# One dense pass inside each P V burst, as eight strip products, in a layer of local attention and a feed-forward gate

## The chip, the cores and the metric

The kernel runs on one core of a Trainium2 chip. The metric is the device time of the whole program in microseconds; a kernel's time is the median of its runs. Beside it stands one execution taken by the hardware profiler, whose span (first to last instruction of the program) and rows are quoted.

## The reference

One layer over 2048 tokens of width 448, in bf16. x is normalized to xn. Branch A is causal attention with 16 heads of 28 over eight positions two apart, the token's own and seven before it; branch B is a feed-forward layer of width 1792 with gelu. The result is x plus the product of the first with silu of the second:

```python
qkv = (xn @ wqkv).reshape(B, S, 3, H, Dh)
idx = pos[:, None] - 2 * arange(8)[None, :]          # masked where negative
attn = softmax(einsum("bhsd,bhswd->bhsw", q, k[idx]) * Dh ** -0.5)
s = einsum("bhsw,bhswd->bhsd", attn, v[idx]) @ wo
g = silu(gelu(xn @ w1 + b1) @ w2 + b2)
return x + s * g
```

## The kernel before, in words

**Tokens and stages.** Tokens of even and odd position are kept apart, so that the neighbours two apart lie side by side; there are 16 tiles of 128 tokens in 4 chunks of 4 tiles. For each tile: statistics and normalization (L422 to L507), a transposed copy xnT, projections to q, k (`qk_rows`, L569) and v (`vproj`, L592). For each chunk: ff1 (`ff1`, L645), that is 14 row tiles of the hidden layer over 512 tokens, evacuated by ScalarE with gelu (L655); ff2 (`ff2`, L671), evacuated into the gate (`gate`, L712). Last the output projection and the gated sum (`final`, L857; `gated`, L881) and the DMA out (L900). For tiles in TWICE (8, 9, 10) that DMA is issued in two halves.

**Attention** goes over nine blocks of up to 228 tokens. A visit S(b) is a *score burst* (`scores_of`, L740): 32 products of 64x128 with 57 columns (L750), then exp on ScalarE (L759) and a mask on VectorE (L765). A visit P(b) is a *P V burst* (`values_of`, L769): 64 products with 57 columns, in the mode in which the 128x128 array stands as eight tiles of 64 rows and 32 columns (L779). Four loops go over s (four quarters of the block), g (column strip of 32), h, and a (row half); so the first 32 products are s = 0 and 1. The row halves write two banks. VectorE then transposes (L791), divides (L795, L799), and turns the result into oT (L816); GpSimd and ScalarE move pieces (L812). Bursts are numbered by their block, 0 to 8.

**The dense pair.** All large products but the first and the last tiles go through `pair` (L514). It takes two jobs a and b (two tiles of the same kind) and runs them beside each other in the two row halves of the array (64x128 mode): a on the upper 64 rows of its contraction with bank p, b on the lower 64 rows with bank q; then the halves are swapped. One *pass* is two such products side by side. A q/k, v or ff1 pair has four passes before the swap and three after, an ff2 pair 7 + 7 and 7 + 7, an output projection three and four. Since after the swap another row half writes into the same bank, the first swapped products wait for a `nop` on GpSimd (`told`, L534), which waits for the last products before the swap (`behind`, L510). The weight slices are `half_rows` (L454).

**The order of the work** is written out by hand. The kernel first makes a list of tasks (`plan.add`), each with an engine, dependencies, and buffers taken and given back (`_Pool`; the eight PSUM banks are `p_b`); `plan.run` places them in the sequence of the list ORDER (a negative number takes the task's second engine), with a cost model that only fixes which free buffer a task gets; `plan.emit` issues them in that sequence, each engine's queue in its own part of it. A pool `p_f` with a CLK task of 3.5 keeps P V bursts apart in the plan. TensorE's task for a P V burst is made in `attn` (L838, task at L849).

Of the kernel before, what the change touches and what calls it, by code (L numbers as in the profile page):

```python
# [13 lines left out]
HOP = 0.10  # L14
TABLE = 1.28
SWITCH = 0.095
AT_ONCE = ("DMA", "CLK")
BURST = 3.5
ORDER = [
# [42 lines left out]
]  # L62
LAST = 352
TWICE = (8, 9, 10)
# [126 lines left out]
def kernel(  # L191
# [13 lines left out]
    P = 128  # L205
# [308 lines left out]
    def pair(a, b, early=False, before=(range(4),), after=(range(3),), late=((),), give=()):  # L514
        held, size = {}, sum(map(len, before)) + sum(map(len, after))

        def part(j, ps, kt, half, n):
            return lambda: j.part(ps, kt, half, n == 0, n == size - 1)

        n, t = 0, None  # L520
        for i, ks in enumerate(before):
            def f1(k, ks=ks, n=n):
                p, q = buf(p_b, t, 0), buf(p_b, t, 1)
                held["last"] = together([part(a, p, kt, 0, n + m) for m, kt in enumerate(ks)], [part(b, q, kt, 1, n + m) for m, kt in enumerate(ks)])[-1]
            u = plan.add("PE", pe(a.n, len(ks)), f1, (list(late[i]) + [u] if i else a.deps + b.deps + a.late + b.late),
                         take=() if i else (p_b, p_b) + a.into + b.into, tail=0.15, mode=64)
            t = t or u
            n += len(ks)
# [7 lines left out]
        for i, ks in enumerate(after):  # L536
            def f3(k, ks=ks, n=n, i=i):
                p, q = buf(p_b, t, 0), buf(p_b, t, 1)
                for x in together([part(b, q, kt, 0, n + m) for m, kt in enumerate(ks)], [part(a, p, kt, 1, n + m) for m, kt in enumerate(ks)])[0]:
                    if not i:  # L540
                        behind(x, held["told"])
            u = plan.add("PE", pe(a.n, len(ks)), f3, [u if i else told], give=give if i + 1 == len(after) else (), tail=0.15, mode=64)
            n += len(ks)
# [25 lines left out]
    def qk_rows(t, which):  # L569
        cs = slice(t * P, (t + 1) * P)  # L570

        def part(ps, kt, half, start, stop):
            r = half_rows(half)
            w = w_in[r, kt, which * D:(which + 1) * D] if kt < 3 else w_in3[r, 0, :]
            return nc.tensor.matmul(ps[:, :D], xnT[r, kt, cs], w, start=start, stop=stop)  # L575
# [16 lines left out]
    def vproj(t):  # L592
        k0 = t * P

        def part(ps, kt, half, start, stop):
            r = half_rows(half)
            w = w_in[r, kt, 2 * D:] if kt < 3 else w_in3[r, 1, :]
            return nc.tensor.matmul(ps[:, :D], xnT[r, kt, k0:k0 + P], w, start=start, stop=stop)  # L598
# [46 lines left out]
    def ff1(c, mt, gate):  # L645
# [3 lines left out]
        def part(ps, kt, half, start, stop):  # L649
            r = half_rows(half)  # L650
            return nc.tensor.matmul(ps[:], w1[r, kt, ms], xnT[r, kt, cs], start=start, stop=stop)  # L651
# [19 lines left out]
    def ff2(t):  # L671
# [5 lines left out]
        elif t % 2 == 0:  # L677
            def job(t):
                cs = slice(t % TPC * P, t % TPC * P + P)

                def part(ps, mt, half, start, stop):
                    r = half_rows(half)
                    return nc.tensor.matmul(ps[:, :D], buf(*h_at[(c, mt)])[r, cs], w2[r, mt, :], start=start, stop=stop)  # L683
# [384 lines left out]
```

## Time and profile before

| what | us |
|---|---|
| runs | 150.19, 150.27, 150.95 |
| median | 150.27 |
| the profiled execution | 150.79 |
| its span | 149.1 |
| TensorE busy in the span | 144.4 |
| VectorE, ScalarE, GpSimd busy | 107.0, 102.9, 27.8 |

In the profile PE is TensorE's products, PEld its weight loads, DVE VectorE, ACT ScalarE, POOL GpSimd, SP the engine that issues most DMAs; L651 is line 651 of the kernel. Times are in microseconds unless marked ns. A group's row has the engine, the operation, the tiles written and read, their shapes and the count, then busy time and the mean of one in ns. Rows of a timeline give the start, the length up to the end of the last instruction, and the count. The start of a product is recorded; its end is modelled.

### The profile page before, as it was taken

The numbers are of one execution on the slowest core, as the hardware profiler recorded it, in microseconds if no ns is written. First come the engines' busy times: TensorE is split into PE (matmuls) and PEld (weight loads), VectorE is DVE, ScalarE is ACT, GpSimd is POOL, SyncE is SP. The second block draws the span as 40 slices with busy tenths as digits, with TensorE's granted clock in tenths as the row PEclk, the third lists the DMA queues.
The fourth block names the chain that finished last, engine by engine and source line by source line (L and its number), as shares of the span: only waits on it lengthen the run. The fifth ranks groups of instructions, "written<-read, shape, count | busy, mean of one in ns | idle before, by whom it ended". The sixth has DMA issues, their size and how long they took to land.

```text
span 149.1 us, 5240 instructions
## 1 busy us (share of the span) xinstructions
PE 144.4 (97%) x2158; PEld 74.5 (50%) x2158; DVE 107.0 (72%) x271; ACT 102.9 (69%) x187; POOL 27.8 (19%) x84
## 2 busy tenths in 40 slices
PE   7899999999999999999999999999999999999991
PEld 2445444444455555556555655445565444454461
DVE  2775640635545877975997897997979969899473
ACT  3255996878779687937968687988974588642720
POOL 6123230005174002314101011041020210200000
PEclk9999999999999999999999999999999999999999
DMA  4999996998857958699875587520303001030122
GB/s 153 306 280 323 194 133 166 228 346 171 103 99 179 154 129 96 201 163 198 214 85 131 169 115 177 109 65 6 91 22 94 2 4 31 1 95 31 31 66 64
DMA packets 39222, 19.47 MB, mean 131 GB/s; under 512 B 25815, under 2 KB 38586, under 8 KB 39198
## 3 DMA queue, kind: packets, MB, share of 16 engines
q1 hardware_dynamic: 38510, 18.10, 58.9%
q0 software_dynamic: 544, 0.91, 2.4%
q8 instruction: 17, 0.28, 0.8%
q10 hardware_dynamic: 144, 0.11, 0.3%
q14 instruction: 7, 0.06, 0.1%
HBM read 9.42 MB, written 3.94 MB: 90 GB/s over the span
## 4 chain that ended last, share of the span: by engine, by line
PE 94%; DMA 2%; DVE 2%; issue 0%; ACT 0%
PE bank L651 29%; PE bank L683 25%; PE bank L575 15%; PE bank L598 7%; PE bank L867 6%; PE bank L779 4%; PE bank L705 4%; PE bank L750 3%; DMA x_sb<-in_A_x_dram 2%; PE bank L875 1%; DVE st L424 1%; PE bank L499 1%; DVE xn L464 0%; DVE sg L887 0%; ACT w_in L724 0%
## 5 line engine op out<-in xcount | busy, mean ns | idle before, releaser
L651 PE MATMUL bank<-xnT,w 64*128 64x512 bf16 x392 | 44.8, 376 | 0.0
L655 ACT ACTIVATE h<-bank,b 128x512 bf16<-128x512 f32 x56 | 35.4, 690 | 8.1 <-PE bank L651 6.8
L683 PE MATMUL bank<-w,h 64*128 64x448 bf16 x392 | 39.9, 349 | 0.0
L651 PEld LDWEIGHTS <-w 64*128 64x128 bf16 x392 | 18.7, 94 | 22.2
L683 PEld LDWEIGHTS <-h 64*128 64x128 bf16 x392 | 18.3, 94 | 16.3
L575 PE MATMUL bank<-w_in,xnT 64*128 64x448 bf16 (+1 forms) x212 | 25.8, 349 | 0.0
L759 ACT ACTIVATE E<-bank 128x456 bf16<-128x456 f32 (+1 forms) x36 | 17.5, 554 | 3.7 <-PE bank L750 3.6
L313 ACT CAST qk_tok<-bank 128x448 bf16<-128x448 f32 x27 | 13.4, 536 | 7.1 <-PE bank L575 5.0
L424 DVE BATCH_NORM_STATS2 st<-x_sb 128x6 f32<-128x448 bf16 x16 | 9.6, 609 | 10.4 <-DMA x_sb<-in_A_x_dram 10.4
L791 DVE STREAM_TRANSPOSE wide<-bank 128x512 f32<-128x512 f32 x18 | 12.3, 702 | 5.1 <-PE bank L779 5.1
L575 PEld LDWEIGHTS <-xnT 64*128 64x128 bf16 (+1 forms) x212 | 10.6, 94 | 10.2 <-issue 0.8
L812 POOL COPY wide<-wide 64x64 bf16<-64x64 bf16 x23 | 6.6, 305 | 47.4 <-PE bank L651 19.3
L598 PE MATMUL bank<-w_in,xnT 64*128 64x448 bf16 (+1 forms) x106 | 13.6, 350 | 0.0
L816 DVE STREAM_TRANSPOSE oT<-wide 128x512 bf16<-128x512 bf16 x18 | 12.2, 694 | 0.7 <-POOL wide L812 0.5
L464 DVE TENSOR_SCALAR xn<-x_sb,mv,rstd 128x448 bf16<-128x448 bf16 x16 | 6.1, 391 | 8.2 <-POOL rstd L446 8.0
L765 DVE TENSOR_TENSOR E<-E,m_gen 128x456 bf16<-128x456 bf16 (+1 forms) x32 | 11.7, 378 | 0.1
L717 DVE TENSOR_TENSOR wide<-bank,b 128x448 f32<-128x448 f32 x15 | 8.9, 615 | 3.9 <-PE bank L683 2.2
L867 PE MATMUL bank<-wo,oT 64*128 64x448 bf16 x98 | 11.6, 349 | 0.0
L799 DVE TENSOR_TENSOR wide<-wide,rd 128x448 bf16<-128x448 f32 x18 | 11.2, 626 | 0.4
L635 ACT ACTIVATE kd<-qkT,head 128x1024 bf16<-128x1024 bf16 x10 | 11.2, 1157 | 0.0
L313 ACT CAST v_tok<-bank 128x448 bf16<-128x448 f32 x13 | 6.6, 537 | 4.6 <-issue 3.9
L729 ACT ACTIVATE wide<-wide 128x448 f32<-128x448 f32 x12 | 7.0, 579 | 3.2 <-DVE wide L717 3.1
(81 smaller groups left out, 138.9 us busy)
## 6 DMA issues: line engine op xcount, KB each, us to landing
v<-v_hbm SPq DMA_DIRECT2D x16, 128.0 KB, 2.8
v_hbm<-v_tok SPq DMA_DIRECT2D x15, 128.0 KB, 3.6
w<-in_B_w_dram SPq DMA_DIRECT2D x2, 672.0 KB, 7.8
out_dram<-o SPq DMA_DIRECT2D x12, 112.0 KB, 1.7
w_in<-in_A_wqkv_dram SPq DMA_DIRECT2D x3, 336.0 KB, 5.4
x_sb<-in_A_x_dram SPq DMA_DIRECT2D x4, 224.0 KB, 2.7
w<-in_B_w_dram SPq DMA_DIRECT2D x2, 448.0 KB, 5.5
w<-in_B_w_dram SPq DMA_DIRECT2D x2, 336.0 KB, 6.3
```

The lines of the kernel that those rows point to most:

```text
L313: nc.scalar.copy(o, i)
L575: return nc.tensor.matmul(ps[:, :D], xnT[r, kt, cs], w, start=start, stop=stop)
L598: return nc.tensor.matmul(ps[:, :D], xnT[r, kt, k0:k0 + P], w, start=start, stop=stop)
L635: nc.scalar.activation(dst, src, ACT.Copy, scale=head[:, a:a + 1])
L651: return nc.tensor.matmul(ps[:], w1[r, kt, ms], xnT[r, kt, cs], start=start, stop=stop)
L655: nc.scalar.activation(buf(p_h, own, i)[:], buf(p_b, own, i)[:], ACT.Gelu_apprx_tanh, bias=b1[:, mt:mt + 1])
L683: return nc.tensor.matmul(ps[:, :D], buf(*h_at[(c, mt)])[r, cs], w2[r, mt, :], start=start, stop=stop)
L759: nc.scalar.activation(buf(p_E, k)[:, :8 * n], buf(p_b, a, at + i)[:, :8 * n], ACT.Exp, scale=SCALE)
L765: nc.vector.tensor_tensor(out=E, in0=E, in1=m[:, :, :, :n].rearrange("p i g q -> p (i g) q"), op=ALU.mult)
L791: nc.vector.transpose(buf(p_dt, k)[:], buf(p_b, po, a)[:])
L816: nc.vector.transpose(oT[:, a::2, q:q + 256], turned_in(d[a]).rearrange("p l b c -> p l (b c)"))
L867: return nc.tensor.matmul(ps[:, :D], oT[r, kt, t * P:(t + 1) * P], wo[r, kt, :], start=start, stop=stop)
```

## The change

One pass of nine dense pairs is taken out of its pair's task and issued between the second and the third quarter (s = 2) of a P V burst, in P V's own tiling mode: each of its two 64x128 products becomes four products of 64x32, one for each column strip (`product` with a strip, `strips` in `pair`). The strips of the two row halves alternate, so eight products fill the eight tiles of the array; they write 32 partitions each of the pair's two banks. The table INSIDE says for each burst from which pair the pass comes, whether from before or after the swap (0 or 1), and from which part: burst 0 the first pass of tile 8's q/k pair, burst 1 the first swapped pass of the v pair of tiles 10 and 11, burst 2 the same of ff2's tiles 2 and 3, burst 3 the first pass of the second part of ff2's tiles 6 and 7, bursts 4, 7 and 8 the first swapped pass of an ff1 pair, bursts 5 and 6 the first pass of ff2's tiles 8 and 10.

Where that pass is the pair's first, a HOLD task without cost takes the pair's two banks ahead of the burst. Where it is the first after the swap, the first two strip products carry the wait for `told`. The pair's remaining passes come behind the burst, or, if the pass isn't the pair's first, the earlier part ahead of it. The burst's task keeps its cost of 0.52 in the plan; the pair's task is planned with a pass less.

ORDER is another list of 922 entries throughout. TWICE becomes empty, so tiles 8, 9 and 10 go out in one DMA each. The diff, without ORDER and with the repeated edits of `part` shown once:

```diff
+INSIDE = {
+    0: (("qk", 8), 0, 0), 1: (("v", 10), 1, 0), 2: (("ff2", 2), 1, 0), 3: (("ff2", 6), 0, 1), 4: (("ff1", 2, 1), 1, 0),
+    5: (("ff2", 8), 0, 0), 6: (("ff2", 10), 0, 0), 7: (("ff1", 3, 2), 1, 0), 8: (("ff1", 3, 6), 1, 0),
+}
...
-TWICE = (8, 9, 10)
+TWICE = ()
...
-    def pair(a, b, early=False, before=(range(4),), after=(range(3),), late=((),), give=()):
+    def product(ps, n, lhsT, rhs, start, stop, strip=None):
+        rows = slice(0, P) if strip is None else slice(32 * strip, 32 * strip + 32)
+        return nc.tensor.matmul(ps[rows, :n], lhsT[:, rows], rhs, start=start, stop=stop)
+
+    t_pv, in_pv, ahead_of_pv, behind_pv = {}, {}, {}, {}
+
+    def put_inside(b, deps, fn):
+        in_pv[b] = fn
+        if b in t_pv:
+            t_pv[b].deps += deps
+            return [t_pv[b]]
+        ahead_of_pv[b] = deps
+        return None
+
+    def pair(a, b, name, early=False, before=(range(4),), after=(range(3),), late=((),), give=()):
         held, size = {}, sum(map(len, before)) + sum(map(len, after))
...
+        def strips(t, kt, n, swap):
+            x, y = (b, a) if swap else (a, b)
+            p, q = buf(p_b, t[0], int(swap)), buf(p_b, t[0], 1 - int(swap))
+            return [i for j in range(4) for i in together([part(x, p, kt, 0, n, j)], [part(y, q, kt, 1, n, j)])[0]]
...
         for i, ks in enumerate(before):
+            deps = list(late[i]) + [u] if i else a.deps + b.deps + a.late + b.late
+            take = () if i else (p_b, p_b) + a.into + b.into
+            visit, wait = places.get((0, i)), None
+            if visit is not None:
+                if not i:
+                    t = plan.add("HOLD", 0.0, None, deps, take=take, tail=-HOP)
+                    deps, take = [t], ()
+                wait = put_inside(visit, deps, lambda kt=ks[0], n=n: strips(own, kt, n, False))
+                deps, ks, n = wait or [], ks[1:], n + 1
...
         for i, ks in enumerate(after):
+            deps = [u if i else told]
+            visit, wait = places.get((1, i)), None
+            if visit is not None:
+                def f(kt=ks[0], n=n, i=i):
+                    for x in strips(own, kt, n, True)[:2]:
+                        if not i:
+                            behind(x, held["told"])
+                wait = put_inside(visit, deps, f)
+                deps, ks, n = wait or [], ks[1:], n + 1
...
-            return nc.tensor.matmul(ps[:, :D], xnT[r, kt, cs], w, start=start, stop=stop)
+            return product(ps, D, xnT[r, kt, cs], w, start, stop, strip)
...
             for s in range(4):
+                if s == 2 and b in in_pv:
+                    in_pv[b]()
                 for g in range(G):
...
-        a = plan.add("PE", 0.52, lambda k: fn([buf(p_b, k, i) for i in range(2)]), masked + t_v[b] + last_visit[what][-1:],
+        a = plan.add("PE", 0.52, lambda k: fn([buf(p_b, k, i) for i in range(2)]), masked + t_v[b] + last_visit[what][-1:] + ahead_of_pv.get(b, []),
                      take=(p_b, p_b, p_f), give=give, tail=0.15, mode=33)
+        t_pv[b] = a
+        if b in behind_pv:
+            behind_pv[b].deps.append(a)
```

More of the change, by code (lines that the diff above doesn't have):

```diff
@@ L524, in f1 @@
                 held["last"] = together([part(a, p, kt, 0, n + m) for m, kt in enumerate(ks)], [part(b, q, kt, 1, n + m) for m, kt in enumerate(ks)])[-1]
-            u = plan.add("PE", pe(a.n, len(ks)), f1, (list(late[i]) + [u] if i else a.deps + b.deps + a.late + b.late),
-                         take=() if i else (p_b, p_b) + a.into + b.into, tail=0.15, mode=64)
+            u = plan.add("PE", pe(a.n, len(ks)), f1, deps, take=take, tail=0.15, mode=64)
+            if visit is not None and not wait:
+                behind_pv[visit] = u
             t = t or u
+            own[:] = [t]
             n += len(ks)
@@ L536, in pair, with f3 @@
         for i, ks in enumerate(after):
-            def f3(k, ks=ks, n=n, i=i):
+            deps = [u if i else told]
[7 more added lines that the diff above has]
+                deps, ks, n = wait or [], ks[1:], n + 1
+            def f3(k, ks=ks, n=n, i=i, first=not i and visit is None):
                 p, q = buf(p_b, t, 0), buf(p_b, t, 1)
                 for x in together([part(b, q, kt, 0, n + m) for m, kt in enumerate(ks)], [part(a, p, kt, 1, n + m) for m, kt in enumerate(ks)])[0]:
-                    if not i:
+                    if first:
                         behind(x, held["told"])
-            u = plan.add("PE", pe(a.n, len(ks)), f3, [u if i else told], give=give if i + 1 == len(after) else (), tail=0.15, mode=64)
+            u = plan.add("PE", pe(a.n, len(ks)), f3, deps, give=give if i + 1 == len(after) else (), tail=0.15, mode=64)
+            if visit is not None and not wait:
+                behind_pv[visit] = u
             n += len(ks)
@@ L570, in qk_rows, with part @@
         cs = slice(t * P, (t + 1) * P)
-        def part(ps, kt, half, start, stop):
+        def part(ps, kt, half, start, stop, strip=None):
             r = half_rows(half)
             w = w_in[r, kt, which * D:(which + 1) * D] if kt < 3 else w_in3[r, 0, :]
-            return nc.tensor.matmul(ps[:, :D], xnT[r, kt, cs], w, start=start, stop=stop)
+            return product(ps, D, xnT[r, kt, cs], w, start, stop, strip)
         def evac(a, own, i):
@@ L593, in vproj, with part @@
         k0 = t * P
-        def part(ps, kt, half, start, stop):
+        def part(ps, kt, half, start, stop, strip=None):
             r = half_rows(half)
             w = w_in[r, kt, 2 * D:] if kt < 3 else w_in3[r, 1, :]
-            return nc.tensor.matmul(ps[:, :D], xnT[r, kt, k0:k0 + P], w, start=start, stop=stop)
+            return product(ps, D, xnT[r, kt, k0:k0 + P], w, start, stop, strip)
         def evac(a, own, i):
@@ L647, in ff1, with part @@
         ms = slice(mt * P, (mt + 1) * P)
-        def part(ps, kt, half, start, stop):
+        def part(ps, kt, half, start, stop, strip=None):
             r = half_rows(half)
-            return nc.tensor.matmul(ps[:], w1[r, kt, ms], xnT[r, kt, cs], start=start, stop=stop)
+            return product(ps, CH, w1[r, kt, ms], xnT[r, kt, cs], start, stop, strip)
         def evac(a, own, i):
@@ L679, in job, with part @@
                 cs = slice(t % TPC * P, t % TPC * P + P)
-                def part(ps, mt, half, start, stop):
+                def part(ps, mt, half, start, stop, strip=None):
                     r = half_rows(half)
-                    return nc.tensor.matmul(ps[:, :D], buf(*h_at[(c, mt)])[r, cs], w2[r, mt, :], start=start, stop=stop)
+                    return product(ps, D, buf(*h_at[(c, mt)])[r, cs], w2[r, mt, :], start, stop, strip)
                 t_g[t] = []
@@ L689, in ff2 @@
             a.deps = [t_h[(c, mt)] for mt in range(k)] + t_w2[0] + [ff1_last[c]] + ([t_f2[t - 1]] if last else [])
-            u = pair(a, b, False, (range(k), range(k, NMT)), (range(k), range(k, NMT)),
+            u = pair(a, b, ("ff2", t), False, (range(k), range(k, NMT)), (range(k), range(k, NMT)),
                      ((), [t_h[(c, mt)] for mt in range(k, NMT)] + t_w2[1]), tuple(h_at[(c, mt)] for mt in range(NMT)) if last else ())
@@ L864, in job, with part @@
             def job(t):
-                def part(ps, kt, half, start, stop):
+                def part(ps, kt, half, start, stop, strip=None):
                     r = half_rows(half)
-                    return nc.tensor.matmul(ps[:, :D], oT[r, kt, t * P:(t + 1) * P], wo[r, kt, :], start=start, stop=stop)
+                    return product(ps, D, oT[r, kt, t * P:(t + 1) * P], wo[r, kt, :], start, stop, strip)
                 return _Job(D, part, t_oT[t] + t_up.get(t, []) + t_wo + [t_f2[t]], lambda u, own, i: gated(t, slice(0, D), D, t_g[t][0], u, own, i))
-            pair(job(t), job(t + 1), False, (range(3),), (range(KT),))
+            pair(job(t), job(t + 1), ("wo", t), False, (range(3),), (range(KT),))
     def final_part(t, cs, n, g):
@@ L940, in project @@
                 for n in range(2):
-                    pair(*js[n], c < 2)
-                pair(vs[2 * i], vs[2 * i + 1], c < 2)
+                    pair(*js[n], ("qk", t + n), c < 2)
+                pair(vs[2 * i], vs[2 * i + 1], ("v", t), c < 2)
         if c == NCH - 1:
@@ L1023 @@
             for i in range(0, NMT, 2):
-                ff1_last[c] = pair(hs[i], hs[i + 1], c < 2)
+                ff1_last[c] = pair(hs[i], hs[i + 1], ("ff1", c, i // 2), c < 2)
             gels = gels + [t_h[(c, mt)] for mt in range(NMT)]
```

7 lines of the change are left out of this document (4 added, 3 removed), and 84 rows, old and new, of the table ORDER.

## The prediction

> **What bounds the kernel now.** First the page: its head and the chain by engine.
>
> ```profile
> span 149.1 us, 5240 instructions
> ...
> PE 144.4 (97%) x2158; PEld 74.5 (50%) x2158; DVE 107.0 (72%) x271; ACT 102.9 (69%) x187; POOL 27.8 (19%) x84
> ...
> PE 94%; DMA 2%; DVE 2%; issue 0%; ACT 0%
> ```
>
> TensorE is busy for 97% of the span and is 94% of the chain that ended last; the other engines have a quarter or more of their time to spare. So a change is worth what it takes out of TensorE's own row of work, if nothing new makes TensorE wait. The second view is the chain in order of time (start, length, what).
>
> ```profile
> 16.34 8.20 PE bank L651 x76
> ...
> 41.92 3.97 PE bank L683 x42
> 45.89 0.43 PE bank L750 x32
> 46.32 3.97 PE bank L683 x42
> ...
> 53.38 0.76 PE bank L779 x42
> ...
> 64.70 0.63 PE bank L779 x39
> ...
> 121.13 0.63 PE bank L779 x41
> ```
>
> A dense pass is two 64x128 products side by side. So 38 passes of 512 columns take 8.20 us, 0.216 each, and 21 of 448 take 3.97, 0.189 each: these are the prices of a pass. A score burst (L750) takes 0.43; a P V burst (L779) takes 0.63, the first 0.76. There are nine of these. To see what happens in one, I read the timeline of TensorE around the second, then of its weight loads alone, the latter also in the third burst (start, length up to the end of the last, name, count).
>
> ```profile
> 63.97 0.73 PE L575 MATMUL bank<-w_in,xnT 64*128 64x448 bf16 x6
> 64.63 0.32 PE L779 MATMUL bank<-E,v 64*32 64x57 bf16 x32
> 65.26 0.74 PE L598 MATMUL bank<-w_in,xnT 64*128 64x448 bf16 x6
> ...
> 64.63 0.20 PEld L779 LDWEIGHTS <-v 64*32 64x32 bf16 x33 [0.37 <-DMA v<-v_hbm]
> 64.86 0.35 PEld L779 LDWEIGHTS <-v 64*32 64x32 bf16 x31
> ...
> 69.01 0.25 PEld L779 LDWEIGHTS <-v 64*32 64x32 bf16 x33
> 69.24 0.35 PEld L779 LDWEIGHTS <-v 64*32 64x32 bf16 x31
> ```
>
> And the durations of single products (minimum/median/maximum in ns, then first and last start), from the views of the lines:
>
> ```profile
> L779 PE MATMUL bank<-E,v x576: 183/187/199, 53.3 to 129.7; 64*32 64x57 bf16 x171, 64*32 64x56 bf16 x21
> ...
> L683 PE MATMUL bank<-w,h x392: 347/349/361, 41.8 to 136.9; 64*128 64x448 bf16 x196
> ...
> L651 PE MATMUL bank<-xnT,w x392: 376/376/387, 14.7 to 130.2; 64*128 64x512 bf16 x196
> ```
>
> The reader is to see two halves. 33 loads and 32 products, 65 instructions, stand ready: their products start within 0.32 - 0.185 = 0.135 us, 4 ns apart. Then nothing starts until 64.86, 0.23 after the burst's start; from there the other 31 loads take 0.35 - 0.09 = 0.26 to their last start, 8.7 ns for each load with its product, though the array could take them at 4. So TensorE has about 64 instructions in hand, and the rest comes at the pace of its sequencer. The last product starts 0.51 after the first, the next dense pass 0.63 after it. The array has nothing to do for (0.23 - 0.135) + (0.28 - 0.135) = 0.24 of this, and the change puts a pass there.
>
> When does a place come free? In the third burst the 33rd load starts late (69.01 + 0.25 - 0.09 = 69.17), in the second early (64.63 + 0.20 - 0.09 = 64.74); yet in both the 34th starts 0.23 after the burst's first product. That fits the first product's end (0.197, near the row's maximum) plus 0.03, not the moment at which the first 65 have all started. I therefore read that **a place is freed when its product has ended**, in order. This decides the forecast.
>
> **The change part by part.** Time counts from the burst's first product.
>
> *Removed:* nine dense passes, six of 448 columns (bursts 0, 1, 2, 3, 5, 6) and three of 512 (4, 7, 8, of ff1): 6 x 0.189 + 3 x 0.216 = 1.78 us.
>
> *Added:* in each burst eight loads and eight products of 64x32, behind the first 32 products. They stand where the 33rd to 40th product stand now, so the first starts at 0.23 and the last at 0.23 + 7 x 0.0087 = 0.29. The trace has no long product in this mode. Its bounds: all eight abreast, one duration, 0.349 for 448 columns (a dense pass is the same eight strips in two instructions); or fewer abreast. 32 products of 57/448 x 0.187 = 0.024 us of streaming in 0.135 + 0.024 make 0.77/0.16 = 4.8 of eight tiles as a floor on what runs at once; by that a pass takes 8/4.8 = 1.67 times its 0.187, 0.13 us more. I take eight abreast, the row that is nearest in shape being the dense pass; the other end is a rival. The Trainium skill, "TensorE: Matmul & The Clock Gate", section Measured speedup vs the span model, says that products on separate tiles take one product's duration and about 4 ns for each tile. By it the last strip would start 0.03 earlier, and the sum below would be better by nine times that, some 0.3 us; no row here shows long strips, and the 8.7 ns of the second half stand against 4.
>
> *What the burst then costs.* The last P V product stands exactly 64 instructions behind the last strip product (32 loads, 32 products). With places freed at the end it starts at 0.29 + 0.349 + 0.03 = 0.67 instead of 0.51: the burst grows by 0.16 and a pass of 0.189 is gone, a gain of 0.03. For 512 columns: 0.29 + 0.376 + 0.03 = 0.70, growth 0.19, gain 0.216 - 0.19 = 0.03. Over nine bursts **0.25 us** (0.1 to 0.4 with 0.02 of error each). If a place were freed at a product's start, the pace of 8.7 ns alone would count: last start 0.23 + 39 x 0.0087 = 0.57, growth 0.06 (I take 0.07 for 512), gain 6 x 0.13 + 3 x 0.146 = 1.2 us. These are the two ends.
>
> *Waits.* In bursts 1, 2, 4, 7 and 8 the first two strips wait for GpSimd's note that the pair's first half is done. Behind them in TensorE's queue stand the other strips, the second half of P V and all dense work; VectorE's transposes (L791) and the evacuations wait for that. What covers it: at 46.32 above the second half of an ff2 pair follows its first with only a score burst of 0.43 between, without a gap, and the new order has at least that much there (a score burst and half of P V for burst 2, three passes or more for the others). Cost 0; without the cover, the hop. In bursts 0, 5 and 6 the strips open a pair, so two banks must be free by the middle of the burst (HOLD keeps them from an earlier point) and, for 5 and 6, the first gelu tiles; taken as 0, the other end is in the third rival. Burst 3 takes a pass of an open pair, with neither.
>
> *The new order.* Read as text, it keeps the row of TensorE's work, with chunk 1's projections earlier. At the end it changes the tiling mode five times instead of three: tile 14's ff2 goes between the halves of the ff2 pair of tiles 12 and 13, and its output projection between the halves of theirs. The price stands here:
>
> ```profile
> 137.07 0.73 PE L867 MATMUL bank<-wo,oT 64*128 64x448 bf16 x6
> 137.74 2.82 PE L705 MATMUL bank<-w,h 128*128 128x448 bf16 x14
> 140.49 0.93 PE L867 MATMUL bank<-wo,oT 64*128 64x448 bf16 x8
> ```
>
> Three passes of 0.189 are 0.57, and the next begins after 0.67; 14 products are 2.65, and the next begins after 2.75: 0.10 for each change of mode, so 2 x 0.10 = **0.2 us** more. The last instructions behind tile 15 keep their order. One output DMA instead of two for each of tiles 8 to 10 takes three issues from SP, which the chain doesn't hold: 0. The 0.76 of the first burst holds a stall late in its second half that no row explains; I leave its 0.13 where it is.
>
> *Sum:* -0.25 + 0.2 = -0.05 us, on the profiled execution of 150.79 with its span of 149.1, to about 149.0. That execution lies 0.5 over the median of 150.27; on the median the sum gives **150.2 us**. A measurement of this kernel can tell about 0.5% (0.75 us) from no change.
>
> **The rivals.** *Places freed at the start* (faster). For it: depth is counted in instructions, and I infer the freeing from two bursts. Against: the 0.23 that doesn't move with the 33rd load. -1.2 + 0.2: 149.25 us.
>
> *The strips don't run eight abreast* (slower). At 4.8 abreast each burst's last strip ends 0.13 later (0.14 for 512), and with it the last P V product: 0.03 - 0.13 and 0.03 - 0.14 make 6 x 0.10 + 3 x 0.11 = 0.9 lost, plus 0.2: 151.4 us. It decides as soon as the strips need 0.03 more than one duration, that is below 0.187/0.217 x 8 = 6.9 abreast. For it: nothing here shows more than 4.8. Against: that is an average with a ramp, and loads paced it.
>
> *A wait inside the burst or in the new order* (slower). The present row of work has no gap from 16 us on; a new one of 922 entries may have some. A bank or gelu tile late by one evacuation of 0.55 to 0.7 us (page: L313 536 ns, L655 690 ns) in two or three places costs 1.0 to 2: about 151.5 us.
>
> ```profile
> L655 ACT ACTIVATE h<-bank,b 128x512 bf16<-128x512 f32 x56 | 35.4, 690 | 8.1 <-PE bank L651 6.8
> ...
> L313 ACT CAST qk_tok<-bank 128x448 bf16<-128x448 f32 x27 | 13.4, 536 | 7.1 <-PE bank L575 5.0
> ```
>
> **How the numbers follow.** Forecast 50% (its own range 149.8 to 150.7, all within 0.5%); freed at the start 25% (149.0 to 149.5, faster by over 0.5%); fewer abreast 10% and waits 15% (151.0 to 152, slower). So faster 0.25, same 0.5, slower 0.25. The range 149.1 to 151.2 leaves out under a fifth, more of it above.
>
> **What would show it.** The weight loads of a burst: 33, then a gap to 0.23, then the strips' eight 8.7 ns apart. Right, if the last few P V products come in a group of their own near 0.6 to 0.7, and the next dense pass 0.79 after the burst's start (0.82 with 512). If they run through and the pass comes at 0.69, places are freed at the start; if at 0.9, the strips don't run abreast. TensorE's idle rows with a releaser would show the waits, and five steps of 0.10 after 135 us the changes of mode. A first burst of 0.92 instead of 0.79 would be its stall again.

## The result, and the profile after

The changed kernel takes **151.57 us** in the median beside 150.66 of the kernel before, a ratio of 1.007 (95% interval 1.0042 to 1.0099): slower by 0.7%, and above the range of 149.1 to 151.2. The profiled execution took 151.40 us (before 150.79). Ratios leave out executions at a lower granted clock, among them one of the changed kernel's six (154.44 us at 0.989) and the profiled one of best_2, below, whose trace is therefore not used. The page's head:

```profile
span 149.5 us, 5350 instructions
...
PE 144.4 (97%) x2211; PEld 75.2 (50%) x2211; DVE 105.9 (71%) x269; ACT 105.2 (70%) x189; POOL 30.7 (21%) x89
...
PE 93%; DVE 2%; DMA 2%; issue 1%; ACT 1%; ACTq 0%
```

TensorE is still the bound, but ScalarE (ACT) now stands in the chain with 1%. The timelines of the second burst in the changed kernel, products first, then weight loads (start, length up to the end of the last, count):

```profile
64.95 0.32 PE L829 MATMUL bank<-E,v 64*32 64x57 bf16 x32
65.18 0.42 PE L520 MATMUL bank<-w_in,xnT 64*32 64x448 bf16 x8
65.37 0.47 PE L829 MATMUL bank<-E,v 64*32 64x57 bf16 x32
65.77 0.36 PE L520 MATMUL bank<-w_in,xnT 64*128 64x448 bf16 x2
...
64.95 0.20 PEld L829 LDWEIGHTS <-v 64*32 64x32 bf16 x32 [0.37 <-issue]
65.09 0.24 PEld L520 LDWEIGHTS <-xnT 64*32 64x32 bf16 x8
65.25 0.47 PEld L829 LDWEIGHTS <-v 64*32 64x32 bf16 x32
65.77 0.11 PEld L520 LDWEIGHTS <-xnT 64*128 64x128 bf16 x4
```

The strips start 0.23 after the burst, P V goes on at 0.42, and the next dense pass comes 0.82 after the burst's start. That is what a burst of 0.63 and a pass of 0.189 took one after the other. So the bursts give almost nothing and take nothing. The loss stands elsewhere, in the timeline of the changed kernel's score bursts of blocks 6 (104.01) and 7 (105.77), with ScalarE's rows of the same time below:

```profile
104.01 0.59 PE L798 MATMUL bank<-qkT,kd 64*128 64x57 bf16 x32
104.44 1.49 PE L520 MATMUL bank<-w,h 64*128 64x448 bf16 x14
105.77 0.19 PE L798 MATMUL bank<-qkT,kd 64*128 64x57 bf16 x1
106.36 0.81 PE L798 MATMUL bank<-qkT,kd 64*128 64x57 bf16 x31 [0.41 <-ACT E L807]
107.01 0.35 PE L520 MATMUL bank<-w,h 64*128 64x448 bf16 x2
...
101.40 1.26 ACT L703 ACTIVATE h<-bank,b 128x512 bf16<-128x512 f32 x2 [0.23 <-PE bank L520]
104.47 1.28 ACT L807 ACT_TABLE_LOAD   x1 [1.81 <-PE bank L798]
105.76 0.99 ACT L807 ACTIVATE E<-bank 128x456 bf16<-128x456 f32 x2
```

One product of block 7's burst starts at 105.77, the other 31 wait for ScalarE's exp; the burst takes 107.01 - 105.77 = 1.24 instead of 0.43, **0.81 lost**. ScalarE's last gelu had ended at 102.66. Then ScalarE waited 1.81 us for block 6's score burst, and only behind that wait came the load of the exp table, 1.28 us, so that block 6's banks were read from 105.76 on. In the kernel before, the same load came right behind the last gelu, and block 7's burst came 4.40 us after block 6's (108.86 and 104.46) instead of 1.76:

```profile
102.44 1.26 ACT L655 ACTIVATE h<-bank,b 128x512 bf16<-128x512 f32 x2
103.71 1.28 ACT L759 ACT_TABLE_LOAD   x1
105.01 1.44 ACT L759 ACTIVATE E<-bank 128x456 bf16<-128x456 f32 x3
...
104.46 0.59 PE L750 MATMUL bank<-qkT,kd 64*128 64x57 bf16 x32
...
108.86 0.59 PE L750 MATMUL bank<-qkT,kd 64*128 64x57 bf16 x32
```

The rest of the difference of the two traces is small. At the end there are five changes of mode instead of three. Two of them in the changed kernel:

```profile
140.29 0.73 PE L520 MATMUL bank<-wo,oT 64*128 64x448 bf16 x6
140.95 0.93 PE L928 MATMUL bank<-wo,oT 128*128 128x448 bf16 x4
141.81 0.93 PE L520 MATMUL bank<-wo,oT 64*128 64x448 bf16 x8
```

Three passes of 0.189 are 0.57 and the next group begins after 0.66; four products are 0.76 and the next begins after 0.86. From the first of the eight output products at 134.02 (133.67 before) to the start of TensorE's last product, the changed kernel takes 0.21 longer. And 0.13 is gained since the late stall of the first burst is gone.

From the first ff1 pass (14.74 before, 14.45 now) to the start of the last product (145.72 and 146.29) the changed kernel takes 0.86 longer. The spans differ by only 0.46, because this execution reached its first ff1 pass 0.30 earlier and ended 0.10 sooner after its last product.

### The profile page after: what moved, and what is told of

It reads as the page before. It is cut to its first block, busy times and chain, and to the rows that moved or that the text cites. A ratio compares the mean times of both kernels' runs of the same rounds, so it can differ in the third digit from the quotient of the medians.

```text
span 149.5 us, 5350 instructions
## 1 busy us (share of the span) xinstructions
PE 144.4 (97%) x2211; PEld 75.2 (50%) x2211; DVE 105.9 (71%) x269; ACT 105.2 (70%) x189; POOL 30.7 (21%) x89
## 4 chain that ended last, share of the span: by engine, by line
PE 93%; DVE 2%; DMA 2%; issue 1%; ACT 1%; ACTq 0%
PE bank L520 81%; PE bank L753 4%; PE bank L829 3%; PE bank L798 2%; DMA x_sb<-in_A_x_dram 2%; PE bank L928 1%; DVE st L428 1%; PE bank L503 1%; ACT E L807 0%; DVE E L813 0%; DVE xn L468 0%; PE bank L751 0%; DVE sg L940 0%; ACT g L772 0%; PE bank L332 0%
## 5 line engine op out<-in xcount | busy, mean ns | idle before, releaser
L520 PE MATMUL bank<-xnT,w 64*128 64x512 bf16 (+1 forms) x410 | 45.8, 376 | 0.0
L520 PE MATMUL bank<-w,h 64*128 64x448 bf16 (+1 forms) x416 | 41.2, 350 | 0.0
L520 PE MATMUL bank<-w_in,xnT 64*128 64x448 bf16 (+2 forms) x330 | 35.8, 350 | 0.0
L520 PEld LDWEIGHTS <-w 64*128 64x128 bf16 (+1 forms) x410 | 19.2, 94 | 21.6
L520 PEld LDWEIGHTS <-h 64*128 64x128 bf16 (+1 forms) x416 | 18.8, 93 | 16.0 <-issue 0.4
L520 PEld LDWEIGHTS <-xnT 64*128 64x128 bf16 (+2 forms) x330 | 16.2, 94 | 15.1 <-issue 0.6
L862 POOL COPY wide<-wide 64x64 bf16<-64x64 bf16 x26 | 7.7, 304 | 60.5 <-PE bank L520 27.3
L683 ACT ACTIVATE kd<-qkT,head 128x1024 bf16<-128x1024 bf16 x11 | 12.5, 1154 | 0.0
L942 DVE SCALAR_TENSOR_TENSOR sg<-bank,g 128x448 bf16<-128x448 f32 x12 | 7.4, 614 | 2.2 <-PE bank L520 1.9
L829 PEld LDWEIGHTS <-v 64*32 64x32 bf16 x576 | 6.2, 91 | 3.1 <-issue 2.7
```

The costliest lines, as they stand in the source:

```text
L520: return nc.tensor.matmul(ps[rows, :n], lhsT[:, rows], rhs, start=start, stop=stop)
L683: nc.scalar.activation(dst, src, ACT.Copy, scale=head[:, a:a + 1])
L829: nc.tensor.matmul(banks[a][32 * g:32 * g + 32, c0:c0 + n], buf(*v_at[b])[r, s, 2 * g + h, :], buf(p_E, exps[2 * h + s // 2])[r, c1:c1 + n ...
```

## The experiments

Each kernel was timed beside the kernel before on the same chip. The ratio compares the executions of the two and stands with its 95% interval; it need not be the quotient of the two medians (for the changed kernel 1.007, where 151.57 / 150.66 is 1.006). Two ratios less than 0.003 to 0.004 apart can't be told apart; for such differences the traces decide.

| kernel | median, us | before beside it | ratio |
|---|---|---|---|
| table_early | 150.52 | 150.41 | 1.0006 (0.9996 to 1.0015) |
| score_later | 151.34 | 150.41 | 1.0064 (1.0049 to 1.0079) |
| dense_behind | 151.72 | 150.41 | 1.0085 (1.0070 to 1.0101) |
| after_40 | 151.07 | 150.41 | 1.0042 (1.0024 to 1.0060) |
| after_24 | 151.22 | 150.53 | 1.0057 (1.0031 to 1.0083) |
| after_16, after_48 | 151.59, 151.37 (one run each) | 150.53 | |
| tail | 152.74 | 150.37 | 1.0169 (1.0144 to 1.0193) |
| best | 151.63 | 150.37 | 1.0090 (1.0064 to 1.0117) |
| tail_2 | 151.38 | 150.41 | 1.0054 (1.0031 to 1.0077) |
| best_2 | 150.07 | 150.41 | 0.9966 (0.9950 to 0.9982) |
| old_order | 151.06 | 150.38 | 1.0044 (1.0024 to 1.0065) |
| old_order_40 | 150.82 | 150.38 | 1.0027 (1.0003 to 1.0051) |
| old_no_0, old_no_3 | 150.52, 150.76 (one run each) | 150.44 | |

The theory after the result: the strips are neutral, because a place in TensorE's queue is freed only when its product has ended, and the loss is a late exp table in the new order. The rival: the strips cost time, and the waits only show it.

### table_early: the exp table ahead of the score burst

```diff
                 nc.scalar.activation(buf(p_h, own, i)[:], buf(p_b, own, i)[:], ACT.Gelu_apprx_tanh,
                                      bias=b1[:, mt:mt + 1])
+                if (c, mt) == (2, 12):
+                    nc.scalar.activation(sd[:, :1], eps_t[:], ACT.Exp)
```

> The changed kernel with one more instruction: an exp of 128 x 1 on ScalarE right behind the last gelu of chunk 2, so that the exp table is loaded there and not behind the score burst of block 6. Order and strips stay. Theory (a late table): the last gelu ends at 102.7, the table is there by 104.0, block 6's four exps run from 104.5, so that the banks that the next score burst (at 105.77) takes are free at 105.1 and 105.6; its 0.81 us of waiting goes, and the time falls by 0.8, to 150.8 beside the changed kernel's 151.6. Rival (the row of work is too dense there whatever ScalarE does): the wait only moves to a later burst, and the time falls by less than 0.2.

The timeline of the same stretch, ScalarE first:

```profile
102.68 1.28 ACT L706 ACT_TABLE_LOAD   x1
103.97 0.20 ACT L706 ACTIVATE sd<-eps_t 128x1 f32<-128x1 f32 x1
104.48 0.99 ACT L809 ACTIVATE E<-bank 128x456 bf16<-128x456 f32 x2 [0.30 <-PE bank L800]
...
105.77 0.59 PE L800 MATMUL bank<-qkT,kd 64*128 64x57 bf16 x32
106.20 1.11 PE L520 MATMUL bank<-w,h 64*128 64x448 bf16 x10
```

The table is there at 103.97, the exps run from 104.48, and block 7's burst takes its 0.43 without a wait. The ratio falls from 1.007 to 1.0006. The median's distance to the kernel before falls from 0.91 to 0.11 us, 0.80 where 0.8 were expected, and later rows lie 0.82 earlier than in the changed kernel's trace. The rival, that the wait moves to a later burst, is out. With one instruction more, the changed kernel equals the kernel before: this wait is its loss.

### score_later: the same cause from the other side

```diff
-    834, 801, 754, 827, 751, 752, 828, 830, 831, 755, 835, 837, 602, 829, 603, 838, 984, 985,
+    801, 754, 827, 751, 752, 828, 830, 831, 755, 602, 829, 603, 984, 985, 834, 835, 837, 838,
```

Task 834 is block 7's score burst, 801 ff2's swapped part, 984 the output projection.

> The changed kernel with the score burst of block 7 moved behind ff2's first swapped part of tiles 8 and 9 and the first part of the output projection of tiles 6 and 7 (1.9 us later), its exps behind it; the late table stays. Late table and early burst together (theory): banks are free by then, 0.8 us less, about 150.8. If the loss came from anything else in the new order, it stays at 151.6. A new wait for the swap's note (the score burst no longer stands between the two parts) or a later P V burst 7 can take back 0.1 to 0.3.

The burst waits no longer, but the ratio falls only to 1.0064. TensorE's and VectorE's rows show two new waits:

```profile
104.76 3.10 PE L511 MATMUL bank<-w,h 64*128 64x448 bf16 x28
107.69 0.73 PE L511 MATMUL bank<-wo,oT 64*128 64x448 bf16 x6
108.26 0.59 PE L789 MATMUL bank<-qkT,kd 64*128 64x57 bf16 x32
...
110.50 0.61 DVE L756 TENSOR_TENSOR wide<-bank,b 128x448 f32<-128x448 f32 x1
...
110.86 0.09 PEld L820 LDWEIGHTS <-v 64*32 64x32 bf16 x2 [0.37 <-issue]
...
111.16 0.19 PEld L820 LDWEIGHTS <-v 64*32 64x32 bf16 x28 [0.21 <-issue]
```

14 passes that follow each other across the swap take 107.69 - 104.76 = 2.93 instead of 14 x 0.189 = 2.65: 0.28 for GpSimd's note, which the score burst had covered. And P V burst 6 starts its second product, the one for the other bank, at 111.16 instead of 110.87, just after VectorE's bias add (110.50 + 0.61 = 111.11) has left an ff2 bank: 0.29. The profile names no releaser there; the cause is read from the times. Both together leave 0.81 - 0.28 - 0.29 = 0.24 of gain; the trace has 0.27. The expectation had 0.1 to 0.3 for one such wait; two came, 0.57 together. In the traces, taking the cause away was worth three times as much as moving its victim (0.82 and 0.27). The ratios 1.007 and 1.0064 alone couldn't tell this gain from none.

### dense_behind: no strips, the pass behind the burst

```diff
-            return [i for j in range(4) for i in together([part(x, p, kt, 0, n, j)], [part(y, q, kt, 1, n, j)])[0]]
+            return together([part(x, p, kt, 0, n)], [part(y, q, kt, 1, n)])[0]
...
-                if s == 2 and b in in_pv:
-                    in_pv[b]()
                 for g in range(G):
...
+            if b in in_pv:
+                in_pv[b]()
         return fn, tuple((p_E, e, 0) for e in exps) + (v_at[b],)
```

> The changed kernel, same order, but the pass taken from each pair is issued as two dense 64x128 products right behind the last P V product instead of as eight strips in the middle. Theory (the strips hold places in TensorE's queue until they have ended, so that a strip pass costs what a dense one costs): each burst takes 0.63 + 0.19 or 0.22 again against 0.82 or 0.84, so the time is the same within 0.1; the late stall of the first burst may come back for 0.13 more. Rival (strips do hide a pass each, and the time is lost elsewhere): 6 x 0.189 + 3 x 0.216 = 1.8 us slower than the changed kernel.

From the first burst on, this trace and the changed kernel's keep their distance but for 0.05 us over nine bursts. Strips or two dense products: the same, as the theory had it; the rival had 1.8 us. (The ratios, 1.0070 and 1.0085, lie within each other's intervals; this profiled execution also reached its first dense pass 0.68 later.) The first burst has no late stall here either, without strips in its middle. So the 0.13 gained in the first burst isn't the strips' doing.

### after_40, after_24, after_16, after_48: where the strips stand

```diff
-                if s == 2 and b in in_pv:
-                    in_pv[b]()
                 for g in range(G):
+                    if (s, g) == (2, 2) and b in in_pv:
+                        in_pv[b]()
```

The other three have (1, 2), (1, 0) and (3, 0) there, for 24, 16 and 48 products.

> The changed kernel with the eight strips behind 40 products of the burst instead of 32 (before g = 2 of s = 2). Theory (64 places, each free when its product has ended): no P V product is then 64 instructions behind a strip, so all run through, the last at about 0.58 after the burst's start; the first dense load stands 64 behind the first strip's, which ends at 0.30 + 0.35, so the next dense pass starts at about 0.70 instead of 0.82: 0.12 less in each burst, 1.05 in nine, 150.5. Rival (the strips' own end, or fewer than eight abreast, sets the next pass): strips start 0.07 later, so the next pass does too: 0.6 slower, 152.2. Rival (places free at the start): no difference between 32 and 40.

> The changed kernel with the strips behind 24 products of the burst (before g = 2 of s = 1), so that they are among the 64 instructions that stand ready. Theory (64 places, freed when a product has ended; and, from the run with 40, the P V products behind the strips are held until the first strip has streamed for 0.19 and then run 6 ns apart): strips start at 0.10 to 0.13, P V goes on at 0.30, the last 16 products wait for the strips' places until 0.10 + 0.35 + 0.03 = 0.48 and then come at 8 ns, the last at about 0.60, the next dense pass at 0.72, 0.10 less than with 32, 0.9 in nine bursts: 150.7. Rival (the burst ends so long after the strips' start whatever stands behind them): 0.12 earlier strips, next pass at 0.70, 150.5. Rival (the strips cost a pass of the array wherever they stand): 0.82 as with 32, 151.6.

> The same with the strips behind 16 products. Theory: strips at 0.07 to 0.10, P V goes on at 0.26; the places of the strips are free at 0.07 + 0.35 + 0.03 = 0.44, and 24 more products come behind that at 6 to 8.7 ns: the last at 0.58 to 0.65, the next pass at 0.70 to 0.77. Rival (so long after the strips' start): 0.67. Rival (a pass of the array wherever it stands): 0.82.

> The same with the strips behind 48 products. Theory: strips at 0.37 to 0.43, no place is waited for; the 16 products behind them are held until 0.57 and run 6 ns apart, the last at 0.66, the next pass at 0.78. Rival (so long after the strips' start, with 0.46 from the run with 40): 0.83. Rival (a pass of the array wherever it stands): 0.82.

The third burst in each trace, in us from its first product, from the start of single products:

| strips behind | first strip | P V goes on | last P V product | next dense pass |
|---|---|---|---|---|
| 16 | 0.065 | 0.254 | 0.652 | 0.770 |
| 24 | 0.094 | 0.293 | 0.639 | 0.757 |
| 32 (the change) | 0.224 | 0.413 | 0.699 | 0.818 |
| 40 | 0.300 | 0.497 | 0.640 | 0.758 |
| 48 | 0.367 | 0.563 | 0.651 | 0.769 |

The rows for 40 and for 24, products of the third burst:

```profile
69.99 0.47 PE L829 MATMUL bank<-E,v 64*32 64x57 bf16 x38
...
70.32 0.38 PE L520 MATMUL bank<-w,h 64*32 64x448 bf16 x6
70.49 0.33 PE L829 MATMUL bank<-E,v 64*32 64x57 bf16 x24
70.75 0.55 PE L520 MATMUL bank<-w,h 64*128 64x448 bf16 x3
```

```profile
69.77 0.28 PE L829 MATMUL bank<-E,v 64*32 64x57 bf16 x21
...
69.89 0.38 PE L520 MATMUL bank<-w,h 64*32 64x448 bf16 x6
70.06 0.53 PE L829 MATMUL bank<-E,v 64*32 64x57 bf16 x40
70.52 0.55 PE L520 MATMUL bank<-w,h 64*128 64x448 bf16 x4
```

32 is the worst place of the five: only there do the burst's last eight products stand 64 instructions behind the eight strips. Everywhere else the pass grows the burst by 0.124 to 0.137 (0.757 to 0.770 against 0.633) instead of 0.185. The rivals don't fit. With 40, later strips didn't make the next pass later, and 32 and 40 did differ. Of the later ones, "so long after the strips' start" would give 0.67, 0.70 and 0.83 with 16, 24 and 48, and "a pass wherever it stands" 0.82 throughout. The theory rightly put 32 last, but its sizes only fit in part: 0.70 was expected with 40 and 0.72 with 24, and 0.758 and 0.757 were found. What it lacked with 40 is in the third column: P V products behind the strips are held until 0.19 to 0.20 after the first strip's start, as long as a strip streams, and then come 6 ns apart or slower. In the changed kernel's bursts with 512 columns it is 0.215, again the price of a pass (0.216). Over the nine bursts the traces gain 0.52 with 40 and 0.50 with 24. By the ratios it is 0.42 and 0.2, too little to tell from none, but their intervals hold the traces' 0.5.

### tail, then tail_2: the end with three changes of mode

```diff
-    938, 944, 945, -884, 939, 1017, ..., 1028, 946, 940, 942, 947, 1029, 1030, 1031, 1018, 941, 25, 1019, ..., 1026,
+    938, -884, 939, 1017, 944, 945, ..., 946, 940, 942, 947, 1018, 941, 25, 1019, ..., 1026, 1028, 1029, 1030, 1031,
```

944, 945 and 1028 are tile 14's ff2 and output projection, 946 its bias add on VectorE, 940 and 942 those of tiles 12 and 13, 1017 and 1019 their output projection.

> The changed kernel with tile 14's ff2 moved behind the first part of the output projection of tiles 12 and 13, and its output projection behind the second part of theirs, as before the change: three changes of mode at the end instead of five. Theory (0.10 for each change of mode): 0.19 less, 151.4 beside the changed kernel's 151.6. Rival (the changes of mode lie beside waits at the end): the same time.

Up to 142.4 us the trace gains 0.21, and then it loses more than that: the kernel is 1% slower than the changed one. VectorE's row and TensorE's last:

```profile
140.86 1.69 DVE L756 TENSOR_TENSOR wide<-bank,b 128x448 f32<-128x448 f32 x3 [1.49 <-PE bank L744]
...
146.53 0.33 PE L919 MATMUL bank<-wo,oT 128*128 128x96 bf16 x4 [0.51 <-DVE sg L931]
```

The edit moved TensorE's tasks and left VectorE's list as it was. There 946 stood ahead of 940 and 942, so the bias adds of tiles 12 and 13, ready 1.5 us before, waited for tile 14's ff2, which now came later. tail_2 puts 940 and 942 ahead of 946, and ScalarE's 941 and 943 ahead of 947; GpSimd's note 1018 also moves ahead, behind 1017.

> The run before this one moved only TensorE's tasks; VectorE's bias add of tile 14 stayed ahead of those of tiles 12 and 13, which then waited 1.5 us for tile 14's ff2. Here VectorE's and ScalarE's tasks at the end are put in the kernel before's order too (bias adds of 12, 13, then 14; silu of 14 last). Theory (the price is 0.10 for each change of mode, and the loss was that queue): 0.2 less than the changed kernel, 151.4, or 1.4 less than the first try. Rival (the end is bound by what follows the silu, whatever the order): between the two, over 151.8.

Now the gain stays to the end: 0.21 in the trace for two changes of mode. The ratio is 1.0054, in the right direction but too near 1.007 to show it alone.

### best, then best_2: the three together

best has table_early's exp, strips behind 40, and tail's order.

> Three edits on the changed kernel together: the early exp table, the strips behind 40 products, the end with three changes of mode. Theory (they lie in different places on TensorE's row of work and add up): 0.9 + 0.5 + 0.2 = 1.6 less than the changed kernel, 150.0, some 0.3 to 0.4% below the kernel before. Rival (a wait that one of them hides comes back for another): 150.5, no different from before.

The ratio is 1.009: tail's loss is in it. best_2 has tail_2's order instead.

> The early exp table, the strips behind 40 products, and the mended end together. Theory (the three add up): 0.9 + 0.5 + 0.2 less than the changed kernel's 151.6, so 150.0, 0.3% below the kernel before. Rival (the bursts' gain is taken back by a wait behind them): 150.5, no different from before.

The ratio is **0.9966** (0.9950 to 0.9982), with 150.07 where 150.0 was expected: the three effects add up, and this version is faster than both kernels, though only by 0.3% than the kernel before. Against table_early's 1.0006 the ratio is 0.004 lower, so the other two edits together are clear of noise too.

### old_order and its variants: strips without the new order

These kernels have the kernel before's ORDER, renumbered, and its TWICE, with eight strip passes in the same bursts (burst 6 stays whole); old_order_40 places them behind 40 products.

```diff
-ORDER = [
-    126, 64, 62, 82, 60, 54, 1, 2, 49, 50, ...
+ORDER = [
+    53, 49, 50, 126, 1, 82, 64, 54, 56, 52, ...
...
-    5: (("ff2", 8), 0, 0), 6: (("ff2", 10), 0, 0), 7: (("ff1", 3, 2), 1, 0), 8: (("ff1", 3, 6), 1, 0),
+    5: (("ff2", 8), 0, 0), 7: (("ff1", 3, 2), 1, 0), 8: (("ff1", 3, 6), 1, 0),
```

> The kernel before with its own order and eight of the nine strip passes (burst 6 stays whole, since two banks are not free ahead of it there), behind 32 products as in the change. Theory (strips behind 32 products cost what a pass costs; the loss lies in the order): 8 x 0.004 less, and the stall of 0.13 in the first burst may go: 150.2 to 150.4 beside 150.4. Rival (strips lose time that the new order gains back): over 150.9.

> The same with the strips behind 40 products. Theory: 0.06 less in each of eight bursts, 149.8 to 149.9, 0.3% below the kernel before, without anything of the new order. Rival (the gain of 40 shows only where the new order leaves room): 150.4.

Both came out slower than the theory, at 1.0044 and 1.0027, and old_order's 151.06 is the number of its rival. But the strips lose no time in the trace: most bursts are what they were (next pass at 0.815 and 0.758), and only in burst 5 the second product starts 0.09 late. The time goes in one stop in the middle of a row of ff2 passes, here old_order:

```profile
85.98 0.54 PE L511 MATMUL bank<-w,h 64*128 64x448 bf16 x4
86.99 2.45 PE L511 MATMUL bank<-w,h 64*128 64x448 bf16 x24 [0.47 <-issue]
```

The third pass was due at 86.36 and started at 86.99; in old_order_40 it came 0.82 late, at the same instruction. "issue" says that nothing the profile shows was waited for. Two more kernels leave out the strips of burst 0 or of burst 3:

> The strips in the old order without those of burst 0, so that TensorE has 12 instructions fewer ahead of the stop at 86.2 us. If the stop belongs to the count of instructions (its code comes in pieces), it moves to 12 instructions later in the work, three passes further on, or goes. If it belongs to the pair of tiles 6 and 7, whose pass is in burst 3, it stays behind that pair's second swapped pass, 0.6 to 0.8 us long.

> The strips in the old order without those of burst 3. If the stop belongs to the pair of tiles 6 and 7, it is gone. If it belongs to the count of instructions, it moves by three passes or goes, as without burst 0.

```profile
86.12 2.81 PE L511 MATMUL bank<-w,h 64*128 64x448 bf16 x28
```

This is old_no_0: 28 products without a stop, and 150.52 beside 150.44; old_no_3 has none either, with 150.76. The stop doesn't belong to the pair whose pass was moved, since it also goes when another burst's strips are left out. It goes with 12 instructions fewer ahead of it (a strip pass is 16 instructions, a dense one 4), which fits code that arrives in pieces; that was not shown directly, and stays open. Without the stop, strips behind 32 products in the old order take about the kernel before's time, as the theory says: single runs are 0.08 and 0.32 slower, and from the first ff1 pass to the last product the two traces are 0.03 and 0.10 shorter than the kernel before's.

## Why the prediction was wrong, step by step

**What bounds the kernel**: right. TensorE is 93% of the changed kernel's chain (94% before).

**Removed, 1.78 us**: right. Dense passes keep 0.189 and 0.216 from the changed kernel's rows.

**Strips**: right in time and number. They start at 0.224 to 0.293, against 0.23 to 0.29. All eight run abreast: P V goes on 0.189 after the first strip, one stream of a dense pass. The rival of fewer abreast is out. The strips come 0.069 / 7 = 9.9 ns apart behind 32 products, and 6 ns apart (0.094 to 0.138 us in the first burst) behind 24, where they are among the instructions that stand ready. The 4 ns for each tile of the Trainium skill, "TensorE: Matmul & The Clock Gate", section Measured speedup vs the span model, are not reached here by either; the kernel before's P V products that stand ready do come 4 ns apart (32 within 0.135).

**A place is freed when its product has ended**: right. In the second burst of the changed kernel the 57th P V product starts 0.597 after the burst, that is 0.224 + 0.346 + 0.027, the end of the strip 64 instructions ahead and 0.027 more; in a burst with 512 columns, whose strips take 372 ns instead of 346, it is 0.624. The five places of the strips bear it out: with 16, the 64th instruction behind the first strip starts at 0.439, again 0.065 + 0.347 + 0.027; with 24 it starts at 0.493, 0.013 after that sum. The rival of places freed at the start (25%) is out.

**What the burst then costs**: the right mechanism, mis-sized. The forecast let the last product start when the last strip's place is free, 0.67; it starts at 0.699, since the last eight products come 14 ns apart (0.597 to 0.699), not 8.7; why is open. The next pass comes at 0.82 instead of the 0.79 foretold. These 0.03 in each of nine bursts were the whole gain: measured are 0.003 for 448 columns (0.189 - (0.816 - 0.630)) and 0.007 for 512 (0.216 - (0.842 - 0.633)), **0.04 in all instead of 0.25**.

**First burst**: its stall of 0.13 was left in place and went away; dense_behind shows that strips aren't needed for that. old_no_0, with the old order and burst 0 whole, still has half of it (next pass at 0.696 instead of 0.763). Why it goes is open. That it went here was luck for the sum.

**Waits, taken as 0**: this is the step that failed. Inside the bursts none came, in nine of nine. But the forecast gave the new order nothing beyond 0.2 at the end, and in it one bank came late: 0.81 at block 7's score burst. The text weighed a wait in the new order as a rival, with 15% and 151.5 us; it was the case, with another cause than named: not an evacuation of 0.55 to 0.7 late in two or three places, but one table load behind a wait for TensorE. That its 151.5 lies so near 151.57 is chance: it stood 1.2 over a median of 150.27, and the change cost 0.91 beside 150.66. What could have been read ahead: the row of the load in the kernel before (1.28 us, between the last gelu and the first exp) and the distance of the two score bursts, 4.40 us there, one ff2 part in the new order.

**End, +0.2**: right. The trace has five steps of 0.09 to 0.10 and 0.21 more at the end, and tail_2 takes 0.21 back. The three output DMAs that are issued in one piece instead of two were taken as 0; that wasn't tried alone.

**Sum**: -0.04 - 0.13 + 0.81 + 0.21 = +0.85 us against -0.05. The traces differ by 0.86 from the first ff1 pass to the last product, and the medians by 0.91. Without the wait the sum is +0.04, which is what table_early's trace has over the same stretch.

## What to carry to other kernels

Before work is put into an idle gap, count the instructions between the long ones put in and the last short ones behind them: at the depth of the queue (64 here) the short ones wait for the long ones' end, and a shift by eight products was worth 0.06 in each burst. When the order of work is changed along with it, look at what was hidden in the old order by distance alone (a table load, a bank's evacuation, a note between engines) and put the distance in the new order beside its length. And move a task on all engines' lists, not on one: tail cost 1.4 us more than tail_2.

## What the runs showed of the hardware

**A table load can wait with its exp.** In the changed kernel the load stood idle behind the exp's wait for TensorE while ScalarE had nothing to do for 1.81 us; a first exp of 128 x 1 elements, with no such wait, had it done by 103.97. Both traces have a separate instruction that waits for a semaphore (EVENT_SEMAPHORE) ahead of the load. In the changed kernel it ended at 104.44, released by the score burst, and the load started at 104.47. In the kernel before it ended at 103.28, before that burst began (104.46), so it wasn't the wait for TensorE; that one came behind the load. Why the compiled programs differ in this wasn't tried. The Trainium skill, "ScalarE: Activation LUTs", section What ACT_TABLE_LOAD costs, has 1283 ns for the load and about 1380 ns for a drain, 2.66 us in all. The traces agree with the load (1.28) but show no such drain: in the kernel before, the load starts 0.02 after the last gelu's end and the next activation 0.01 after the load.

**Two places of wait in one burst.** A short product behind a long one on the same tile is held for the long one's stream (0.19 to 0.20 after its start), and the 64th instruction behind it for its end (0.35 and 0.03 more). Only the runs with the strips at other places show the two apart.

**Code in pieces.** The changed kernel's page lists a queue for instructions:

```profile
q8 instruction: 17, 0.28, 0.8%
```

17 packets of 0.28 MB are 16 KB each. The Trainium skill, "Runtime: NRT & Kernel Launch", section Instruction fetch mechanics, says that an engine's code is refilled in blocks of 16 KiB, 256 instructions, and mostly hidden. The size agrees; that the stop of 0.64 to 0.82 in the old order is such a refill is not shown. In old_order the last such packet ahead of the stop ran from 84.30 to 85.66, and so had ended before the third pass was due at 86.36.

**The same start varies.** The eleven kernels with the new order whose traces are used have the same start, and reached their first product on 64 rows between 9.27 (tail) and 10.70 us (best). The latest is best, where TensorE waited for the weights:

```profile
7.87 0.35 PE L511 MATMUL bank<-w_in,xnT 128*128 128x448 bf16 x1 [1.23 <-DMA w_in<-in_A_wqkv_dram]
```

So the spans of two profiled executions say little on a difference of some tenths; traces of the new order were compared from the first burst on.
